# A longer pause of MLP work between a batch's first stage and its middle stage

## The chip, the cores and the metric

The kernel runs on one core of a Trainium2 chip. The metric is the device time of one execution in microseconds (us). A core has a matrix engine (TensorE, PE in the profile, its weight loads PEld), a vector engine (VectorE, DVE), a scalar engine (ScalarE, ACT), GpSimd (POOL) and SyncE (SP), which issues DMAs; ScalarE issues some as well.

## The reference

For each of 8 batches a sequence of 3008 tokens of 256 features goes through a Fourier transform, a complex projection with a soft threshold, and the inverse transform; all 24064 tokens then go through an MLP of width 2048 with a leaky ReLU.

```python
X = np.fft.rfft(x, axis=1)                 # x: 8 x 3008 x 256
Yr = Xr @ w_r - Xi @ w_i + b_r
Yi = Xr @ w_i + Xi @ w_r + b_i
Yr = np.sign(Yr) * np.maximum(np.abs(Yr) - lam, 0.0)   # and Yi
y = np.fft.irfft(Y, n=x.shape[1], axis=1)
h = y.reshape(24064, 256) @ w_in           # w_in: 256 x 2048
out = np.maximum(0.01 * h, h) @ w_out      # w_out: 2048 x 256
```

## The kernel before

The transform of 3008 = 47 x 64 points is split into stages. The first stage (`fwd(b)`) transforms along the 47: it loads x, folds it on GpSimd (sum and difference, lines 245 and 246), splits it into a high and a low part (lines 254 and 255), multiplies (line 78, tile psf from xz), copies the result out on ScalarE (line 264) and stores it to a DRAM tile u_dram from ScalarE's queue (line 267). The middle stage (`mid(b)`) loads u from u_dram on SyncE's queue (line 329), transforms along the 64 (line 343, bank psf from fb and u), projects and thresholds (line 78 with wr, wn, wd; VectorE lines 390 to 392), turns back (line 78 with gb) and stores to v_dram. A middle stage has 12 such rounds. The last stage (`inverse`, line 480) loads vin and gives the tokens y, which `forms` turns into seven combinations (yt, yc; lines 509 to 513) with high and low parts (line 505 on ScalarE, line 506 on VectorE).

The MLP takes the tokens in 47 chunks of 512, each in 8 steps, so 376 MLP steps. A step's first product is a seven-product scheme in two halves (`moe_a`, `moe_b`; line 92, banks psh, 21 matmuls of 256 columns) and its second product adds 12 matmuls of 512 columns two steps later (line 576, bank pso). Between the halves VectorE adds up what the first half left in the banks: line 543 (u2), line 545 and line 546 (gf). The third product of the second half writes into a bank that line 546 has read, so TensorE must wait for line 546 there. Line 557 ends the hidden tile gf and line 563 takes its low part gl.

Every matmul is done in three terms (high x high, high x low, low x high). While the MLP of one batch's tokens runs, the transform of a later batch is interleaved: a `Stream` wraps the generator of a stage, whose `yield` values say how many columns of work were just written, and after each half of an MLP step the main loop lets the current streams go on until their share of the whole is reached:

```python
work = frac / 0.95 * sum(s.total for s in streams)
for s in streams:
    s.to(work / s.total)
    work = max(0, work - s.total)
```

For a later batch the two streams are `fwd(b)` and then `mid(b)`. `mid(b)` writes the loads of its first two u tiles and then yields a number with no work behind it (line 424), so that MLP work is written until the stream's share has grown by that number. This is the pause.

All this sets the order in which the instructions are written. The order in which they stand on each engine is made from it by the library's scheduler, which works with a timed model of its own (`schedule_with_timeline_sim=True`); only the MLP's matmuls are tied to each other in their written order (`in_order`). The numbers in tile names count up in the written order.

Of the kernel before, what the change touches and what calls it, by code (L numbers as in the profile page):

```python
# [30 lines left out]
def spectral_mlp_kernel(  # L31
# [17 lines left out]
    NB = x.shape[0]  # L49
# [8 lines left out]
    CS = 512  # L58
# [253 lines left out]
    def mid(b):  # L312
# [13 lines left out]
        def load(j):  # L326
            u = sb.tile([P, 2, D], F32, name="u", tag="u", bufs=3)
            for c in range(2):
                ld = sync.dma_start(u[c * N2:(c + 1) * N2], ud[c, 2 * j:2 * j + 2, :N2, :].rearrange("k n d -> n k d"))
                if b == 0:  # L330
                    reads.append(ld)
            u_t[j] = u
# [88 lines left out]

        for j in range(2):
            load(j)
        yield 6 * CS if b else 0
        if b:
            for s in range(NPAIR):
                if s + 2 < NPAIR:
# [216 lines left out]
    MID = NPAIR * (16 * P + 18 * D + 3 * CS)  # L644
# [37 lines left out]
    with tc.issue_after(turned[0].ins):  # L682
        split_consts()
    m0 = Stream(mid(0), MID)
    m0.to(0.001)
    for c in range(2, 4):
# [28 lines left out]
    next(wout)  # L715


    mids = [Stream(mid(b), MID + 6 * CS) for b in range(1, NB)]
    cur, streams = -1, ()
    for i, pos in enumerate(moe()):  # L720
        if i % 2 == 0 and len(converted) < NQ:
# [121 lines left out]
```

## Time and profile before

| | |
|---|---|
| median of 3 timed runs (range) | 2605.85 us (2603.67 to 2608.62) |
| the profiled execution: time, span | 2600.34 us, 2598.6 us |
| TensorE matmul busy, share of the span | 2537.5 us, 98% |
| VectorE, ScalarE, GpSimd busy | 1897.1 us (73%), 1668.5 us (64%), 229.6 us (9%) |
| mean granted TensorE clock | 0.993 |
| chain that ended last: lines 576, 92, 78 | 38%, 34%, 11% |

The span reaches from the first to the last instruction. A share of busy time is an average over the whole; where a single wait stands, and who ended it, is read from the views of waits, of the chain that ended last, and of the timeline. The granted clock is the share of full speed that TensorE had.

### The profile page before, as it was taken

How to read it: one execution, taken by the hardware profiler on the slowest of the kernel's cores; microseconds unless marked ns; L12 is line 12 of the kernel's file. 1: busy time of each engine (PE TensorE's matmuls, PEld its weight loads, DVE VectorE, ACT ScalarE, POOL GpSimd, SP SyncE). 2: the span in 40 equal slices, each digit the busy share in tenths (PEclk: the TensorE clock that was granted, in tenths of full speed). 3: DMA queues.
4: the chain of work that ended last, by engine and by line, in shares of the span. 5: the costliest groups of instructions: out<-in, count | busy, mean ns of one | idle time of the engine just before them, and what ended most of it. 6: DMA issues, size and time to landing. Idle time of an engine off the chain costs nothing.

```text
span 2598.6 us, 42643 instructions
## 1 busy us (share of the span) xinstructions
PE 2537.5 (98%) x16300; PEld 2281.5 (88%) x16300; DVE 1897.1 (73%) x3403; ACT 1668.5 (64%) x3174; POOL 229.6 (9%) x180
## 2 busy tenths in 40 slices
PE   5999999999999999999999999999999999999999
PEld 4689888999889998899988999889998889999998
DVE  7687786776777778777786777877777777767675
ACT  5766665776556666567665666566666667655564
POOL 0001121100110001100021000210002000000000
PEclk8999999999999999999999999999999999999999
DMA  8621132111221113211132111321113221101000
GB/s 259 179 85 50 48 89 72 54 47 48 82 78 49 45 41 90 75 55 51 33 97 68 49 49 37 104 67 49 49 36 101 64 58 48 44 17 32 9 17 17
DMA packets 119912, 165.13 MB, mean 64 GB/s; under 512 B 13601, under 2 KB 69917, under 8 KB 119709
## 3 DMA queue, kind: packets, MB, share of 16 engines
q1 hardware_dynamic: 79120, 115.55, 14.6%
q10 hardware_dynamic: 40589, 46.87, 7.1%
q8 instruction: 128, 2.10, 0.4%
q14 instruction: 75, 0.61, 0.1%
HBM read 86.60 MB, written 75.76 MB: 62 GB/s over the span
## 4 chain that ended last, share of the span: by engine, by line
PE 89%; DVE 3%; DMA 2%; ACT 1%; issue 0%; ACTq 0%; SPq 0%; DVEq 0%
PE pso L576 38%; PE psh L92 34%; PE psf L78 11%; PE psf L480 3%; PE psf L343 3%; DMA u<-u_dram 1%; DMA u_dram<-xin 1%; DVE yl L506 0%; DVE gl L563 0%; DMA raw<-w_out_dram 0%; DVE gf L557 0%; ACT gh L561 0%; DVE yt L511 0%; ACT gf L559 0%; DVE yc L512 0%
## 5 line engine op out<-in xcount | busy, mean ns | idle before, releaser
L92 PE MATMUL psh<-yh,win_hi 128*128 128x256 f32 x2632 | 752.3, 286 | 13.8 <-DVE gf L546 10.6
L92 PE MATMUL psh<-yl,win_hi 128*128 128x256 f32 x2632 | 738.3, 280 | 0.6 <-DVE yl L506 0.5
L92 PE MATMUL psh<-yh,win_lo 128*128 128x256 f32 x2632 | 737.9, 280 | 0.0
L576 PE MATMUL pso<-gh,wout_hi 128*128 128x512 f32 x1504 | 593.9, 395 | 0.0
L576 PE MATMUL pso<-gl,wout_hi 128*128 128x512 f32 x1504 | 591.1, 393 | 0.5 <-DVE gl L563 0.5
L576 PE MATMUL pso<-gh,wout_lo 128*128 128x512 f32 x1504 | 590.4, 393 | 0.0
L563 DVE TENSOR_TENSOR gl<-gf,gh 128x1024 fp32r<-128x1024 f32 x376 | 471.8, 1255 | 92.7 <-ACT gh L561 90.6
L92 PEld LDWEIGHTS psh<-yh,win_hi 128*128 128x128 f32 x2632 | 497.0, 189 | 30.7 <-DVE gf L546 15.4
L92 PEld LDWEIGHTS psh<-yl,win_hi 128*128 128x128 f32 x2632 | 497.0, 189 | 12.5 <-DVE yl L506 1.0
L92 PEld LDWEIGHTS psh<-yh,win_lo 128*128 128x128 f32 x2632 | 496.6, 189 | 0.2
L557 DVE TENSOR_TENSOR gf<-psh,u 128x512 f32<-128x512 f32 x376 | 259.1, 689 | 256.3 <-PE psh L92 255.1
L561 ACT CAST gh<-gf 128x1024 fp32r<-128x1024 f32 x376 | 396.4, 1054 | 7.1
L559 ACT ACTIVATE gf<-gf 128x768 f32<-128x768 f32 x376 | 320.0, 851 | 49.5 <-DVE gf L557 47.7
L576 PEld LDWEIGHTS pso<-gl,wout_hi 128*128 128x128 f32 x1504 | 282.5, 188 | 62.9 <-DVE gl L563 1.0
L576 PEld LDWEIGHTS pso<-gh,wout_hi 128*128 128x128 f32 x1504 | 283.1, 188 | 46.9 <-ACT gh L561 0.4
L576 PEld LDWEIGHTS pso<-gh,wout_lo 128*128 128x128 f32 x1504 | 282.9, 188 | 44.9
L556 ACT ACTIVATE gf<-psh 128x256 f32<-128x256 f32 x376 | 145.5, 387 | 266.6 <-PE psh L92 246.9
L542 ACT COPY p<-psh 128x256 f32<-128x256 f32 x376 | 140.1, 373 | 220.2 <-PE psh L92 219.1
L379 POOL TENSOR_TENSOR kb<-bias,kc 128x512 f32<-128x512 f32 x84 | 119.0, 1417 | 1530.6 <-ACT kc L376 1409.6
L543 DVE TENSOR_TENSOR u<-psh,p 128x256 f32<-128x256 f32 x376 | 158.6, 422 | 105.8 <-ACT p L542 103.5
L545 DVE TENSOR_TENSOR gf<-psh,u 128x256 f32<-128x256 f32 x376 | 159.3, 424 | 29.7 <-PE psh L92 2.0
L546 DVE TENSOR_TENSOR gf<-psh,gf 128x256 f32<-128x256 f32 x376 | 159.1, 423 | 9.0
(134 smaller groups left out, 3253.2 us busy)
## 6 DMA issues: line engine op xcount, KB each, us to landing
u<-u_dram SPq DMA_DIRECT2D x192, 128.0 KB, 2.7
v_dram<-v ACTq DMA_DIRECT2D x192, 128.0 KB, 2.4
out_dram<-ob SPq DMA_DIRECT2D x94, 256.0 KB, 2.1
vin<-v_dram SPq DMA_DIRECT2D x96, 240.0 KB, 3.5
xin<-x_dram SPq DMA_DIRECT2D x90, 240.0 KB, 3.0
u_dram<-xin ACTq DMA_DIRECT2D x72, 240.0 KB, 2.4
u_dram<-xin SPq DMA_DIRECT2D x24, 240.0 KB, 3.9
raw<-w_out_dram SPq DMA_DIRECT2D x8, 512.0 KB, 5.0
```

The lines of the kernel that those rows point to most:

```text
L78: last = nc.tensor.matmul(dst, a, b, start=(i == 0), stop=(i == len(terms) - 1))
L92: mlp[:] = [nc.tensor.matmul(dst, a, b, start=start and i == 0, stop=i == 2, skip_group_check=True)]
L542: act.copy(p1, b1[:, lo])
L543: dve.tensor_add(u2, b1[:, hi], p1)
L545: dve.tensor_add(g[:, 3], b2[:, hi], u2)
L546: dve.tensor_add(g[:, 3], b2[:, lo], g[:, 3])
L556: act.activation(g[:, 0], b1[:, lo], AF.Prelu, alpha=SLOPE)
L557: dve.tensor_add(g[:, 1:3], b2.rearrange("p (k n) -> p k n", k=2), u2.unsqueeze(1).broadcast_to([P, 2, HT]))
L559: act.activation(g[:, 1:4], g[:, 1:4], AF.Prelu, alpha=SLOPE)
L561: cp = act.copy(gh, g)
L563: parted[:] = [cp, dve.tensor_sub(gl, g, gh.bitcast(F32))]
L576: mlp[:] = [nc.tensor.matmul(po, a[:, f, s], r[:, i], start=(f == 0 and j == 0), stop=(f == NF - 1 and j == 2),)]
```

## The change

The number that `mid(b)` yields between its first loads and its first work goes from 6 x 512 to 9 x 512 columns for every batch but the first, and the total of these streams goes up by as much. Nothing else is changed.

```diff
@@ -421,7 +421,7 @@
 
         for j in range(2):
             load(j)
-        yield 6 * CS if b else 0
+        yield 9 * CS if b else 0
         if b:
             for s in range(NPAIR):
                 if s + 2 < NPAIR:
@@ -715,7 +715,7 @@
     next(wout)
 
 
-    mids = [Stream(mid(b), MID + 6 * CS) for b in range(1, NB)]
+    mids = [Stream(mid(b), MID + 9 * CS) for b in range(1, NB)]
     cur, streams = -1, ()
     for i, pos in enumerate(moe()):
```

Since a scheduler makes the engines' order from the written one, three places of the built order are shown, before and after.

TensorE at the hand-over of the second later batch, from the last first-stage matmuls (fa1) to the first of the middle stage (fb). Before:

```order
L78 MATMUL psf_4147<-xz_4144,fa1_hi_233 120x256
L78 MATMUL psf_4147<-xz_4144,fa1_lo_234 120x256
L92 MATMUL psh_4510<-yh_3805,win_hi_186 128x256
L92 MATMUL psh_4510<-yl_3806,win_hi_186 128x256
...
L576 MATMUL pso_4280<-gh_4398,wout_hi_897 128x512
...
L576 MATMUL pso_4287<-gl_4400,wout_hi_897 128x512
L92 MATMUL psh_4510<-yh_3805,win_hi_186 128x256
L92 MATMUL psh_4510<-yl_3806,win_hi_186 128x256
L92 MATMUL psh_4510<-yh_3805,win_lo_187 128x256
L343 MATMUL psf_4246<-fb_103,u_4182 128x2x64 x4
```

The change:

```order
L78 MATMUL psf_4147<-xz_4117,fa1_hi_233 120x256
L78 MATMUL psf_4147<-xz_4117,fa1_lo_234 120x256
L92 MATMUL psh_4569<-yh_3821,win_hi_186 128x256
L92 MATMUL psh_4569<-yl_3822,win_hi_186 128x256
...
L576 MATMUL pso_4264<-gh_4475,wout_hi_897 128x512
...
L576 MATMUL pso_4287<-gl_4477,wout_hi_897 128x512
L92 MATMUL psh_4569<-yh_3821,win_hi_186 128x256
L92 MATMUL psh_4569<-yl_3822,win_hi_186 128x256
L92 MATMUL psh_4569<-yh_3821,win_lo_187 128x256
L343 MATMUL psf_4274<-fb_103,u_4182 128x2x64 x4
```

Between the pair of line 78 and line 343 stand 9 matmuls of line 92, 12 of line 576 and 3 of line 92 in both; the whole place has moved by one MLP step (psh_4510 is now psh_4569), and the bank of line 343 is written later (psf_4274 for psf_4246).

VectorE in MLP step 77 (near 670 us before), up to line 546. Lines 511, 512, 513 and 506 are the split of the next tokens, 390 to 392 the threshold of a middle stage. Before:

```order
L563 TENSOR_TENSOR gl_6911<-gf_6863,gh_6909 128x1024
L511 TENSOR_TENSOR yt_6913<-yc_6141,yt_6913 128x256
L512 TENSOR_TENSOR yc_6141<-yc_6141 128x256
L391 TENSOR_SCALAR c_6926<-t_6925 128x512
L543 TENSOR_TENSOR u2_6953<-psh_6938,p1_6952 128x256
L506 TENSOR_TENSOR yl_6915<-yc_6141,yh_6914 128x512
L513 TENSOR_TENSOR yc_6141<-yc_6141,yt_6913 128x256
L392 TENSOR_TENSOR t_6925<-t_6925,c_6926 128x512
L506 TENSOR_TENSOR yl_6915<-yt_6913,yh_6914 128x512
L545 TENSOR_TENSOR gf_6956<-psh_6939,u2_6953 128x256
L506 TENSOR_TENSOR yl_6915<-yc_6141,yh_6914 128x512
L546 TENSOR_TENSOR gf_6956<-psh_6939,gf_6956 128x256
```

The change:

```order
L513 TENSOR_TENSOR yc_6141<-yc_6141,yt_6913 128x256
L557 TENSOR_TENSOR gf_6863<-psh_6846,u2_6860 128x512
L506 TENSOR_TENSOR yl_6915<-yc_6141,yh_6914 128x512
L390 TENSOR_TENSOR t_6925<-psf_6884,kb_6802 128x512
L506 TENSOR_TENSOR yl_6915<-yt_6913,yh_6914 128x512
L506 TENSOR_TENSOR yl_6915<-yc_6141,yh_6914 128x512
L391 TENSOR_SCALAR c_6926<-t_6925 128x512
L543 TENSOR_TENSOR u2_6953<-psh_6938,p1_6952 128x256
L563 TENSOR_TENSOR gl_6911<-gf_6863,gh_6909 128x1024
L392 TENSOR_TENSOR t_6925<-t_6925,c_6926 128x512
L545 TENSOR_TENSOR gf_6956<-psh_6939,u2_6953 128x256
L546 TENSOR_TENSOR gf_6956<-psh_6939,gf_6956 128x256
```

The split (lines 513 and 506) has moved from behind line 543 to ahead of it; line 563 now stands behind line 543.

VectorE in MLP steps 123 and 124, at the split of another chunk. Before, in step 124:

```order
L557 TENSOR_TENSOR gf_10365<-psh_10348,u2_10362 128x512
L511 TENSOR_TENSOR yt_10419<-yc_9736,yt_10419 128x256
L512 TENSOR_TENSOR yc_9736<-yc_9736 128x256
L506 TENSOR_TENSOR yl_10421<-yc_9736,yh_10420 128x512
L513 TENSOR_TENSOR yc_9736<-yc_9736,yt_10419 128x256
L543 TENSOR_TENSOR u2_10448<-psh_10433,p1_10447 128x256
L506 TENSOR_TENSOR yl_10421<-yt_10419,yh_10420 128x512
L545 TENSOR_TENSOR gf_10451<-psh_10434,u2_10448 128x256
L563 TENSOR_TENSOR gl_10417<-gf_10365,gh_10415 128x1024
L546 TENSOR_TENSOR gf_10451<-psh_10434,gf_10451 128x256
```

The change, in step 123:

```order
L543 TENSOR_TENSOR u2_10362<-psh_10347,p1_10361 128x256
L511 TENSOR_TENSOR yt_10419<-yc_9736,yt_10419 128x256
L512 TENSOR_TENSOR yc_9736<-yc_9736 128x256
L506 TENSOR_TENSOR yl_10421<-yc_9736,yh_10420 128x512
L545 TENSOR_TENSOR gf_10365<-psh_10348,u2_10362 128x256
L513 TENSOR_TENSOR yc_9736<-yc_9736,yt_10419 128x256
L506 TENSOR_TENSOR yl_10421<-yt_10419,yh_10420 128x512
L546 TENSOR_TENSOR gf_10365<-psh_10348,gf_10365 128x256
```

The split of this chunk stands one step earlier and now lies between line 543 and line 546. The same five rows stand there in steps 29, 196 and 267 too, where before they did not.

## Rows read from the trace of the kernel before

**Rows 1.** Waits of TensorE from 140 us on: total us, times, longest.

```profile
PE psf L343 <- DMA u<-u_dram: 9.6, 6, 2.4
PE psh L92 <- DVE gf L546: 8.9, 8, 2.8
PE psh L92 <- DVE u L543: 2.2, 2, 1.9
```

**Rows 2.** Chain that ended last, 435 to 446 us: start, us, what.

```profile
436.06 1.05 PE psh L92 x9
437.11 0.25 PE psf L78 x2
...
437.39 0.38 ACT xin L264
...
437.80 3.10 DMA u_dram<-xin
...
440.91 2.75 DMA u<-u_dram
...
443.80 1.13 PE psf L343 x8
```

**Rows 3.** The same chain, 446 to 453 us.

```profile
446.24 3.25 PE psh L92 x18
449.49 2.74 PE pso L576 x12
```

**Rows 4.** TensorE in two stretches: us, busy (instructions), granted clock, DMA share, GB/s.

```profile
444.40:447.90 3.50, 3.50 (x22) 0.62 0.36 110
669.70:676.60 6.90, 4.22 (x19) 0.56 0.01 2
```

**Rows 5.** Timeline of TensorE near 670 us; in brackets the idle time before.

```profile
668.98 0.39 PE L92 MATMUL psh<-yh,win_hi 128*128 128x256 f32 x1 [1.91 <-DVE u L543]
...
672.38 0.58 PE L92 MATMUL psh<-yh,win_hi 128*128 128x256 f32 x1 [2.79 <-DVE gf L546]
```

**Rows 6.** Chain that ended last, 660 to 690 us.

```profile
665.41 1.44 DVE yt L511
666.85 1.41 DVE yc L512
...
668.59 0.33 DVE u L543
...
670.46 0.60 DVE yl L506
...
672.38 4.21 PE psh L92 x18
```

**Rows 7.** Timeline of GpSimd, 663 to 673 us.

```profile
664.57 2.00 POOL L245 TENSOR_TENSOR xs<-xin,xin 120x512 f32<-120x512 f32 x1 [9.65 <-DMA xin<-x_dram]
666.64 1.33 POOL L246 TENSOR_TENSOR xin<-xin,xin 120x512 f32<-120x512 f32 x1
```

**Rows 8.** All of line 511: ns least/median/most, first and last start, form.

```profile
L511 DVE TENSOR_TENSOR yt<-yc,yt x47: 412/420/1521, 127.1 to 2519.7; 128x256 f32<-128x256 f32 x47
```

**Rows 9.** Waits of TensorE, 200 to 430 us.

```profile
PE psf L78 <- ACT eh L358: 1.6, 2, 1.1
```

**Rows 10.** Waits of TensorE, 1150 to 1690 us.

```profile
PE psh L92 <- DVE gf L546: 2.0, 2, 1.2
```

**Rows 11.** Waits of TensorE, 2065 to 2120 us.

```profile
PE psh L92 <- DVE gf L546: 1.1, 1, 1.1
PE psh L92 <- DVE yl L506: 0.5, 1, 0.5
PE psf L78 <- ACT eh L358: 0.3, 1, 0.3
```

**Rows 12.** Timeline in an MLP step without a split: line 546, then the product behind it.

```profile
1594.94 0.43 DVE L546 TENSOR_TENSOR gf<-psh,gf 128x256 f32<-128x256 f32 x1
...
1597.70 0.28 PE L92 MATMUL psh<-yh,win_hi 128*128 128x256 f32 x1
```

## The prediction

> **What bounds the kernel now.** I read first who waits on TensorE once the opening 140 us are over. TensorE is the bound: it runs one long row of matmuls, and what can be won lies in the gaps of that row. The list of its waits [rows 1] is short: 9.6 us in six waits of line 343 for the tile u, and 8.9 and 2.2 us in ten waits of the MLP product (line 92) for VectorE's gf and u2 additions. So I look at two places: the hand-over from a batch's first stage to its middle stage, where the pause stands, and the worst VectorE wait.
>
> The hand-over of the second later batch is in the chain of waits [rows 2]: the last first-stage matmuls end at 437.36 (437.11 + 0.25), ScalarE copies them out from 437.39, its store to u_dram lands after 3.10 us, only then can SyncE issue the load of u, which takes 2.75 us, and the first middle-stage matmul starts at 443.80. From 437.36 to 443.80 that is 6.4 us of latency. In that time TensorE had 9 + 3 matmuls of line 92 (1.05 us for nine [rows 2]) and 12 of line 576 (2.74 us for twelve [rows 3]), so 1.05 + 0.35 + 2.74 = 4.1 us, and stood for the rest. The six waits of line 343 are this place in the six later batches. After it the granted clock was 0.62 on average over the next 3.5 us [rows 4], a mix of the 1.2 and 2.4 GHz levels, and 18 matmuls of line 92 took 3.25 us [rows 3] where 18 at 1.05 us for nine take 2.1: 1.1 us more.
>
> The second place is around 670 us. TensorE stood 1.91 and 2.79 us in one MLP step [rows 5], and the chain of waits there runs through VectorE [rows 6]: it did the additions of the inverse transform's split (yt, yc, yl) ahead of and between the additions that TensorE needed. After it the clock was granted at 0.56 over 6.9 us [rows 4], and 18 matmuls took 4.21 us [rows 6], 2.1 us more than 2.1.
>
> **The change, part by part.** It adds no instruction: both orders hold the same matmuls. It adds 3 x 512 = 1536 to the pause that a later batch's `mid` reports and the same to its total.
>
> *The pause itself.* By the code one would expect 3.7% of a stretch where 2.5% stood (4608 of 124928 units, 3072 of 123392), so more MLP between store and use, and the u waits gone. The built order says otherwise. Between the last first-stage matmul and the first of line 343 stand 9, 12 and 3 MLP matmuls before, and 9, 12 and 3 after (first pair of order rows, and the same in all six later batches). The numbers in the names, which count up as the code is written, tell why: in both versions the bank of line 343 (psf_4246, now psf_4274) was written ahead of the MLP bank that executes before it (psh_4510, now psh_4569). The scheduler already holds line 343 back until it believes that u has landed; a pause that ends earlier than that is not seen. So I cost this part at nothing: the six waits stay, 9.6 us, and the 1.1 us of slow clock with them. The bounds are 0 and 9.6 + 1.1 = 10.7 us gained.
>
> *The pacing.* The larger total lets every stretch spread its work a little differently. Counted in the order by MLP steps (376 in all), the attention's instructions move by mostly 0 and at most 2 steps, the last middle stage ends 0.3 step earlier, and the MLP's tail is unchanged. TensorE's work stays; only which VectorE and ScalarE rows meet which MLP step changes. What can change is therefore the waits of line 92 (and those of line 78 for ScalarE) at places whose neighbourhood is reordered.
>
> *What goes.* At these places the rows around the wait are no longer the same: 1.6 us near 312 and 343 us [rows 9], 1.91 + 2.79 us near 670 [rows 5], 2.0 us in two near 1152 and 1683 [rows 10], 1.1 + 0.5 + 0.3 us from 2070 to 2115 [rows 11]. Together 10.2 us, and 2.1 us of slow clock after the pair near 670: 12.3 us. At the largest the new order is plainly kinder (second pair of order rows): before, five attention operations stood between line 543 and line 546; now only lines 563 and 392 do, since the split is done earlier.
>
> *What comes.* TensorE waits when VectorE has much to do between line 543 and line 546 of one step. A step without such work has 2.3 us to spare: line 546 ended at 1594.94 + 0.43 and TensorE wanted it at 1597.70 [rows 12]. I counted in both orders the steps with at least 1.7 us of attention work there, by the durations of its rows. Before there are 12 that are now different, after there are 9 that are new. Of the 12, three waited: the pair near 670 (4.7 us), 1.2 near 1152 [rows 10], 1.1 near 2115 [rows 11], so 7.0 / 12 = 0.58 us a place; without the pair 2.3 / 11 = 0.21. Nine new places then cost 9 x 0.21 = 1.9 to 9 x 0.58 = 5.3 us. Four of the nine are one pattern (third pair of order rows): lines 511, 512, 506, 513 and 506 in that gap, three of 0.33 us (by line 543, which is as wide) and two of 0.60 [rows 6], 2.2 us, about the 2.3 to spare, so near nothing each. I still take 5.3, since what made the dear place dear, below, is not removed by the change. The other waits that go (10.2 - 7.0 = 3.2 us) I let come back in full at other places: they are many small chances that the change draws anew. New waits: 8.5 us. Bounds: 0, and 9 x (4.7 + 2.1) = 61 if each were as dear as the dearest, which the eleven others exclude; three such, 20.4 + 3.2 = 23.6, is as far as I go.
>
> *Why one place was so dear.* The two operations of lines 511 and 512 took 1.44 and 1.41 us on the chain [rows 6], against a median of 0.42 [rows 8]. In just that time GpSimd ran its two additions that fold the next batch's input, 664.57 to 666.57 and 666.64 to 667.97 [rows 7], and each VectorE operation ended 0.3 us behind one of them. That is 2 x 1.05 = 2.1 of the 4.7 us. The Trainium skill (page "SBUF — State Buffer", section "Who interferes with whom") says that a VectorE instruction with two SBUF inputs and a GpSimd one that reads SBUF exclude each other, and that the later one waits until the first has finished. The trace agrees here: the VectorE operations end with GpSimd's, rather than slow down by some share.
>
> The sum against the profiled execution's own time: 2600.34 - 12.3 + 8.5 = 2596.5 us. The three timed runs have a median of 2605.85, 5.5 above that execution, so on them 2605.85 - 3.8 = 2602.05 us.
>
> **The rivals.** (1) *The pause works on the chip as the code reads*: TensorE gets more to do before line 343 and the u waits end: 2605.85 - 10.7 = 2595.2. For it speaks only the code; the order, with the same 24 matmuls between, speaks against it.
> (2) *The dear place goes and nothing like it comes*: the new waits are 1.9 + 3.2 = 5.1, so 12.3 - 5.1 = 7.2 us gained, 2598.7; with no new waits at all 2593.6. For it speaks that the split near 670 is now ahead of line 543, and that four of nine new places fit into the spare time.
> (3) *Slower: the split meets GpSimd again.* Each meeting of a step's split with a fold costs up to 2.1 us on VectorE and, where the spare time is used up already, the whole 4.7 + 2.1 = 6.8 us. Three such places among the nine give 20.4 + 3.2 - 12.3 = 11.3 us, 2617; it is slower than no change by over 0.2% from 12.3 + 5.2 = 17.5 us of new waits. For it speaks that the pattern of line 511 behind line 543 stands in four steps where it stood in none, and uses up the spare 2.3 us; against it that two of the four lie in the midst of a middle stage, where no fold runs. By the rule cited above from the Trainium skill, such a meeting costs all that is left of GpSimd's instruction, so a place is either dear or free; this widens the case and does not move it.
>
> **How the numbers follow.** A timing of this kernel tells about 0.2%, 5.2 us, from no change. Forecast (reordered waits, a net of some -4 us, its own range 2600.6 to 2611): 0.50. Rival 1: 0.05. Rival 2: 0.32, nearly all of it over the 5.2 us. Rival 3: 0.13. So faster 0.37, same 0.50, slower 0.13. The forecast's time is 2602.05; the range leaves out a tenth on each side: from 2594, rival 2 with hardly a new wait, to 2611, where new waits are 17.5 us.
>
> **What would show it.** In the profile after, line 343 should again wait six times for u, about 9 to 11 us in all; if that is under 3 us, rival 1 holds. The pair of waits near 670 us should be gone or under 2 us. The waits of line 92 behind VectorE should sum to 6 to 12 us where 11.1 stood; under 5 is rival 2, over 20 rival 3, with VectorE's lines 509 to 513 at over 1 us beside GpSimd's additions. Wrong would be the whole reasoning if the time moved by over 0.3% with these sums unchanged, for instance by TensorE's clock alone.

## The result: no faster, slightly slower

| | before | change |
|---|---|---|
| median of 16 runs each (range) | 2602.13 us (2600.03 to 2608.62) | 2607.75 us (2604.26 to 2611.39) |
| the profiled execution: time, span | 2600.34, 2598.6 us | 2608.53, 2606.7 us |
| TensorE matmul busy, share of the span | 2537.5 us, 98% | 2541.6 us, 98% |
| mean granted TensorE clock | 0.993 | 0.992 |

The ratio of the two kernels is taken as 1.0018 with a 95% interval of 1.0011 to 1.0026: 4.7 us (0.0018 x 2602) slower, between 2.9 and 6.8; the two medians lie 5.6 us apart. That is under the 0.2% that the prediction took as what a timing can tell, but 16 runs of each tell it from no change. The forecast was 3.8 us faster.

The waits of TensorE in the changed kernel, from 140 us on (total us, times, longest), are to be held against [rows 1]:

```profile
PE psh L92 <- DVE gf L546: 8.2, 8, 2.5
PE psf L343 <- DMA u<-u_dram: 7.1, 6, 1.4
PE psf L78 <- ACT eh L358: 3.5, 4, 1.8
PE psh L92 <- DVE u L543: 2.7, 3, 1.3
PE psh L92 <- DVE yl L506: 2.3, 2, 1.4
PE psf L78 <- DVE eh L359: 0.9, 1, 0.9
PE pso L576 <- DVE gl L563: 0.8, 2, 0.5
PE psf L78 <- ACT v L418: 0.7, 1, 0.7
```

[rows 1] show only the three largest groups of before; the same list of before goes on with

```profile
PE psf L78 <- ACT eh L358: 1.8, 3, 1.1
...
PE psh L92 <- DVE yl L506: 0.5, 1, 0.5
```

and line 576 for gl with 0.5. Line 343 still waits six times for u, and its longest wait is 1.4 us where 2.4 stood. Small groups of before have grown: line 92 for yl, and line 78 for eh, which ScalarE writes (line 358) in the middle stage's own chain of copies. New are line 78 for eh from VectorE (line 359) and for v.

The hand-over of the second later batch, in the chain that ended last (start, us, what), answers to [rows 2]:

```profile
446.55 0.25 PE psf L78 x2
...
447.24 2.15 DMA u_dram<-xin
449.41 2.58 DMA u<-u_dram
452.12 1.13 PE psf L343 x8
```

The same steps take 5.3 us from the last matmul of line 78 (446.80) to the first of line 343, where 6.4 stood; the store landed after 2.15 us instead of 3.10. The work between is the same 24 matmuls in both built orders. Near 670 us, in the chain behind [rows 6], the split is shorter but still there:

```profile
670.10 2.84 DVE yl L506 x2
...
673.28 0.33 DVE u L543
...
675.72 0.44 DVE gf L546
676.20 4.21 PE psh L92 x18
```

Two operations of line 506 take 2.84 us together, where [rows 6] have 0.60 for one, and push line 543 and line 546 back; TensorE waits 0.92 us for the one and 1.91 for the other, 2.8 instead of 4.7 us, and the 18 matmuls behind them still run slowly, in 4.21 us as in [rows 6].

And this is new, at the start of a chunk of tokens; the timeline of TensorE from 460 to 475 us (in brackets the idle time and what ended it) has two waits:

```profile
465.31 0.39 PE L92 MATMUL psh<-yl,win_hi 128*128 128x256 f32 x1 [0.81 <-DVE yl L506]
467.38 0.58 PE L92 MATMUL psh<-yl,win_hi 128*128 128x256 f32 x1 [1.45 <-DVE yl L506]
```

So do the two largest of the late places, TensorE's timeline from 2110 to 2125 and from 2220 to 2234 us:

```profile
2119.45 0.39 PE L78 MATMUL psf<-wr_hi,eh 128*128 128x256 f32 x1 [1.83 <-ACT eh L358]
...
2227.34 0.39 PE L92 MATMUL psh<-yh,win_hi 128*128 128x256 f32 x1 [1.30 <-DVE u L543]
2228.43 0.39 PE L78 MATMUL psf<-wr_hi,eh 128*128 128x256 f32 x1 [0.47 <-ACT eh L358]
2230.32 0.38 PE L78 MATMUL psf<-wn_hi,eh 128*128 128x256 f32 x1 [0.68 <-ACT v L418]
```

**Where the time is.** Line 546 runs once in each of the 376 MLP steps, so its start is a common mark. It starts 3.9 us later in the first step of the changed kernel's profile and 4.6 us later in the eighth (184.14 against 179.55 us). Up to there the engines still run the same order, so that part is between two executions, not between two kernels. In the last step it is 8.2 us later (2593.30 against 2585.07). The change's own part of the profiled pair is so 8.2 - 4.6 = 3.6 us, in line with the timed 4.7. TensorE from the eighth mark to the last (us, busy (instructions), granted clock, DMA share, GB/s), before and with the change:

```profile
179.55:2585.07 2405.52, 2384.55 (x15595) 1.00 0.19 55
184.14:2593.30 2409.16, 2386.89 (x15593) 1.00 0.19 55
```

Its idle time grew by 1.3 us (22.27 for 20.97), as do its waits from 170 us on (22.5 us after, 21.2 before). The other 2.3 us (2386.89 - 2384.55) are busy time: the same matmuls held TensorE longer. The slow clock doesn't explain it, since it costs 5.1 us in both (one minus the granted clock, summed over stretches of 10 us from 170 us on). In the profile a single matmul of line 92 lasts 0.28 us [rows 12], while nine in a row take 1.05 us [rows 2], so short stalls can lie inside busy time; which matmuls took longer, and why, no row shows.

### The profile page after: what moved, and what is told of

Its sections match the earlier page's. It is cut to its first block, busy times and chain, and to the rows that moved or that the text cites. A ratio compares the mean times of both kernels' runs of the same rounds, so it can differ in the third digit from the quotient of the medians.

```text
span 2606.7 us, 42619 instructions
## 1 busy us (share of the span) xinstructions
PE 2541.6 (98%) x16300; PEld 2282.6 (88%) x16300; DVE 1888.5 (72%) x3403; ACT 1662.2 (64%) x3174; POOL 234.6 (9%) x180
## 4 chain that ended last, share of the span: by engine, by line
PE 87%; DVE 3%; ACT 2%; DMA 2%; issue 1%; POOL 0%; ACTq 0%; SPq 0%; DVEq 0%; POOLq 0%
PE pso L576 37%; PE psh L92 33%; PE psf L78 11%; PE psf L480 3%; PE psf L343 3%; DVE yl L506 1%; DMA u<-u_dram 1%; DMA u_dram<-xin 1%; DVE gl L563 0%; ACT gf L559 0%; DVE gf L557 0%; DVE t L390 0%; ACT yh L505 0%; ACT zf L400 0%; ACT yc L493 0%
## 5 line engine op out<-in xcount | busy, mean ns | idle before, releaser
L563 DVE TENSOR_TENSOR gl<-gf,gh 128x1024 fp32r<-128x1024 f32 x376 | 465.2, 1237 | 95.0 <-ACT gh L561 93.5
```

Of the source, the lines that this page charges most:

```text
L563: parted[:] = [cp, dve.tensor_sub(gl, g, gh.bitcast(F32))]
```

## The experiments

Theory A: the pause is a number that changes the written order; the scheduler makes another order from it, and waits go and come at places that have nothing to do with the pause. Then the time follows the list of waits, and other small changes of the numbers move it either way. Theory B: a longer pause costs by itself (MLP work that stands before the middle stage is missing later), so more pause is slower, and its two edits add up. All kernels compute the whole result. Diffs are against the kernel before unless said. The kernels were timed in three groups, each with its own runs of the kernel before, whose medians are 2604.75 us for e1 to e4, 2603.61 for p3 to p24 and 2603.01 for f1 to f4; the ratios are within a group. The waits are those of one profiled execution of each kernel.

| kernel | ratio to before (95%) | waits of TensorE from 170 us on | of these, line 343 |
|---|---|---|---|
| before | 1 | 21.2 us | 9.6 |
| change | 1.0018 (1.0011 to 1.0026) | 22.5 | 7.1 |
| e1: pause alone | 0.9986 (0.9978 to 0.9994) | 18.6 | 7.9 |
| e2: total alone | 0.9977 (0.9969 to 0.9986) | 16.8 | 7.2 |
| e3: first later batch only | 1.0011 (1.0002 to 1.0019) | 24.7 | 8.3 |
| e4: all later batches but the first | 1.0027 (1.0016 to 1.0038) | 24.6 | 9.9 |
| p3: 3 x 512 | 1.0005 (0.9996 to 1.0014) | 21.6 | 9.2 |
| p8: 8 x 512 | 1.0000 (0.9991 to 1.0009) | 21.4 | 9.1 |
| p12: 12 x 512 | 1.0015 (1.0006 to 1.0024) | 22.6 | 6.2 |
| p24: 24 x 512 | 0.9981 (0.9972 to 0.9989) | 16.7 | 2.6 |
| f1: change, other pace | 1.0015 (1.0006 to 1.0024) | 23.4 | 8.0 |
| f3: before, other pace | 0.9996 (0.9987 to 1.0005) | 20.6 | 9.8 |
| f2: change, no additions on GpSimd | 1.0094 (1.0080 to 1.0108) | 32.8 | 8.9 |
| f4: middle stage held back | 1.0009 (1.0000 to 1.0018) | 17.7 | 0.5 |

Over the 14 kernels the ratio and the sum of waits go together with a correlation of 0.93 (0.83 without f2, the farthest of them).

**e1, the pause alone; e2, the total alone.**

```diff
 e1
-        yield 6 * CS if b else 0
+        yield 9 * CS if b else 0
 e2
-    mids = [Stream(mid(b), MID + 6 * CS) for b in range(1, NB)]
+    mids = [Stream(mid(b), MID + 9 * CS) for b in range(1, NB)]
```

> Pause 9 x 512, total left at 6 x 512. Theory A (the order is drawn anew): within 0.25% of before, either sign, with waits of TensorE at places of its own. Theory B (the longer pause costs by itself): 4 to 5 us slower than before.

> Pause left at 6 x 512, total 9 x 512: only the pacing. Theory A: within 0.25% of before, either sign. Theory B: no change to before, within 0.1%.

Measured: 2601.62 us and 2598.81 us. Each half of the change is faster than before, by 0.14% and 0.23%, and both together are slower by 0.18%. Costs that add up can't do that. In e1 the waits of line 343 are 7.9 us, as with the change, so it is not there that the two part. In e2 the place near 670 us is nearly free; the waits of TensorE from 430 to 700 us in e2:

```profile
PE psf L343 <- DMA u<-u_dram: 2.3, 1, 2.3
PE psh L92 <- DVE yl L506: 0.9, 1, 0.9
PE psh L92 <- DVE gf L546: 0.8, 1, 0.8
```

That is 4.0 us, where the same stretch of the changed kernel has 6.3 (2.3 + 1.9 + 1.2 + 0.9) and that of before 7.0 (2.8 + 2.3 + 1.9). In the profiled executions of e1 and e2 the clock costs nothing from 170 us on, by the same sum that gave 5.1 us; the last section says how much of their gain this may be.

**e3 and e4, the change for one group of batches only.**

```diff
 e3
-        yield 6 * CS if b else 0
+        yield (9 if b == 1 else 6) * CS if b else 0
-    mids = [Stream(mid(b), MID + 6 * CS) for b in range(1, NB)]
+    mids = [Stream(mid(b), MID + (9 if b == 1 else 6) * CS) for b in range(1, NB)]
 e4: the same with (6 if b == 1 else 9) in both lines
```

> Pause and total 9 x 512 in the first later middle stage alone, 6 x 512 in the six others. Theory A: what the change loses up to about 500 us (the waits for yl at the start of the seventh chunk, 2.3 us and 1.7 us of slow clock) can come here too, if the order there is the same as in the change: 2 to 5 us slower. Theory B: a seventh of the loss, 0.7 us.

> Pause and total 9 x 512 in the six later stretches, 6 x 512 in the first. Theory A: no waits for yl near 465 us, since that part stands as before; the rest drawn anew, within 0.25% of before. Theory B: six sevenths of the loss, 4 us slower.

Measured: 2607.51 and 2611.36 us, 0.11% and 0.27% slower; their sum of 0.38% is not the change's 0.18%. But place by place they are its two halves. e3 has the change's early waits; its waits of TensorE from 460 to 475 us:

```profile
PE psh L92 <- DVE yl L506: 2.3, 2, 1.5
```

and before's late ones, its waits from 2070 to 2140 us, row for row [rows 11]:

```profile
PE psh L92 <- DVE gf L546: 1.1, 1, 1.1
PE psh L92 <- DVE yl L506: 0.5, 1, 0.5
PE psf L78 <- ACT eh L358: 0.3, 1, 0.3
```

e4 has no wait from 460 to 475 us and the change's late ones; its waits from 2070 to 2140 and from 2220 to 2240 us:

```profile
PE psf L78 <- ACT eh L358: 1.8, 1, 1.8
...
PE psh L92 <- DVE u L543: 1.3, 1, 1.3
PE psf L78 <- ACT v L418: 0.7, 1, 0.7
PE psf L78 <- ACT eh L358: 0.5, 1, 0.5
```

So a wait for VectorE or ScalarE belongs to its piece of the order and comes back to a tenth of a microsecond in another kernel with the same piece. What the place at 460 to 475 us costs can't be read this way: line 546 starts 7.1 us later than before in e3's 49th MLP step and 11.2 us in its 61st, but only 4.8 and 5.7 us in the changed kernel, which has the same two waits and a fall of the clock behind them; e3 has a third wait in between, 1.4 us for eh.

e3 holds a test that is worth more. From the 101st step on its instructions on TensorE, VectorE and ScalarE stand in the same order as those of before, one by one (by line and tile), so that this is one order in two executions. TensorE from the 101st start of line 546 to the last, before and in e3:

```profile
825.07:2585.07 1760.00, 1749.72 (x11448) 1.00 0.18 52
835.96:2595.63 1759.67, 1749.74 (x11448) 1.00 0.18 52
```

The busy time is the same to 0.02 us, so the 2.3 us more of it in the changed kernel is far more than two executions of one order differ by here: it goes with the order, as the waits for VectorE and ScalarE do. The waits for u do not: before has 2.4 us near 1405 us, where its store landed after 3.52 us, and e3 has 1.4 us at the same place of the order (1415 us), with 2.27 us for the store.

**p3, p8, p12 and p24, other lengths.**

```diff
-        yield 6 * CS if b else 0
+        yield 3 * CS if b else 0
-    mids = [Stream(mid(b), MID + 6 * CS) for b in range(1, NB)]
+    mids = [Stream(mid(b), MID + 3 * CS) for b in range(1, NB)]
 p8, p12 and p24: 8, 12 and 24 in both lines
```

> Pause and total of 3 x 512 instead of 6 x 512. Theory A (the time differs only because the order around the MLP steps is drawn anew): within 0.25% of before, either sign; the six waits for u stay at 7 to 10 us in all, since 4.18 us of MLP matmuls stand in the hand-over as before. Theory B (a longer pause squeezes the middle stage, about 1.6 us for each 512 by the change of 4.7 us for three): 4.7 us faster than before, ratio 0.998.

> Pause and total of 8 x 512. Theory A: within 0.25% of before, either sign, and not tied to the change's 0.18%; waits for u at 7 to 10 us. Theory B: 3.1 us slower than before, ratio 1.0012, between before and the change.

> Pause and total of 12 x 512. The built order has 4.72 us of matmuls in the hand-over in five of six later batches where 4.18 stood, so theory A expects the waits for u to fall by about 5 x 0.54 = 2.7 us, to 5 to 7 us, and the time to be within 0.3% of before. Theory B: 9.4 us slower, ratio 1.0036.

> Pause and total of 24 x 512. The built order has 5.61 us of matmuls in five hand-overs where 4.18 stood, so theory A expects the waits for u to fall by 5 x 1.43 = 7 us, to 1 to 3 us, and the time to be 0 to 8 us below before apart from the order drawn anew (ratio 0.995 to 1.001). Theory B: 28 us slower, ratio 1.011.

Measured for 3, 6, 8, 9, 12 and 24 x 512: +0.05, 0, 0.00, +0.18, +0.15 and -0.19%. No trend of B's kind goes through these. What does follow the length is the hand-over, and only from 12 on. In the built order the matmuls between the last of line 78 and the first of line 343 come to 4.18 us in all six later batches at 3, 6, 8 and 9 x 512; to 4.72 us in five of them at 12, and to 5.61 in five at 24. With that the waits of line 343 fall from some 9 us over 6.2 to 2.6. The chain that ended last in p24, 445 to 456 us:

```profile
448.27 0.24 PE psf L78 x2
448.51 0.89 PE psf L480 x8
449.40 1.07 PE psh L92 x9
450.47 1.62 PE pso L576 x7
452.09 0.89 PE psf L480 x8
452.98 1.16 PE pso L576 x5
454.14 1.00 PE psf L343 x8
```

Here the chain stays on TensorE from line 78 to line 343, with 16 matmuls of line 480 in place of three of line 92; where the changed kernel waited, nothing waits. The other waits of p24 went up from 11.6 (21.2 - 9.6) to 14.1 us, so it wins 4.5 of the 7.0 us in waits, and 4.9 us in the timed runs (0.0019 x 2603.6).

**f1 and f3, another pace.** The divisor that sets the share of all stretches moves by a thousandth, in the change (f1) and in the kernel before (f3).

```diff
-        work = frac / 0.95 * sum(s.total for s in streams)
+        work = frac / 0.951 * sum(s.total for s in streams)
```

> The change as it is (pause and total 9 x 512), and the divisor of the pacing 0.951 instead of 0.95, which has nothing to do with the pause. Its order is the change's up to MLP step 12 and differs after it. Theory A (the time comes from the waits that the order draws): ratio anywhere in 0.997 to 1.003, with the waits at 2119 and 2227 us or 465 us there or not there by the order, so probably closer to before than the change is, 1.000 with a spread of 0.002. Theory B (the longer pause costs): 1.0018, as the change.

> Before (pause and total 6 x 512) with the divisor of the pacing 0.951 instead of 0.95. Same order as before up to MLP step 23. Theory A: ratio to before in 0.997 to 1.003, a spread like that of the kernels with another pause. Theory B: 1.000 within 0.0007.

Measured: 1.0015 and 0.9996, as far apart as the change and before. That is what B expects and not what I had hoped for from A: the two loose ends of this redraw did not bring the pair together. It is no proof of B: 1.0015 lies in A's range too, and f1's sum of waits came out near the change's (23.4 and 22.5 us) by other waits. f1 keeps the change's early places, among them the pair of 0.81 and 1.45 us for yl at 466 and 468 us; but near 670 us it has 1.1 us instead of 2.8, none of the waits at 2119 us and of line 92 at 2227, and 1.2 us near 720 and 1.4 near 1520 that the change has not. So f1 doesn't decide. B falls by e1, e2, p8 and p24.

**f2, no additions on GpSimd.** Against the changed kernel, to test the reason that the prediction gave for the dear place:

```diff
-            eng = pool if b else dve
+            eng = dve
-                    pool.tensor_add(kb, bias, kc.unsqueeze(1).broadcast_to([P, 2, D]))
+                    dve.tensor_add(kb, bias, kc.unsqueeze(1).broadcast_to([P, 2, D]))
```

> The change with the folds and the kb additions on VectorE instead of GpSimd: nothing left that VectorE can meet, for about 168 additions more on VectorE. If the meetings make the waits (about half of the 14.6 us behind the opening lie within 8 us behind a slowed VectorE operation), the pair near 675 us falls from 2.8 to under 1 us and the waits apart from u to 6 to 10 us; the time 0 to 8 us below the change, ratio to before 0.999 to 1.002. If the meetings don't matter and the VectorE load does, waits rise over 15 us and the ratio over 1.003.

Measured: 2627.42 us, 0.94% slower. VectorE's busy time grew from 1888.5 to 1953.9 us and the waits to 32.8. The slowed operations are gone: of line 511 none takes over 427 ns, where the changed kernel has one of 1078 and before one of 1521 [rows 8], and of line 563 none over 1227, where the changed kernel has one of 2321. All of line 511 in f2 (ns least/median/most):

```profile
L511 DVE TENSOR_TENSOR yt<-yc,yt x47: 414/418/427, 130.1 to 2546.9; 128x256 f32<-128x256 f32 x47
```

But a wait of 2.7 us for line 546 stays near the place (686.6 us), where under 1 us was expected if the meetings make the waits. The chain that ended last there, from line 543 to line 546:

```profile
683.66 0.42 DVE yc L513
684.08 0.60 DVE t L392
684.68 0.60 DVE yl L506
685.29 0.33 DVE gf L545
685.62 0.60 DVE yl L506
686.22 0.34 DVE gf L546
```

Four operations of the attention at their usual length, 2.22 us (0.42 + 3 x 0.60), stand between line 543 and line 546 and make up most of the 2.7 us. The meeting with GpSimd makes operations longer; that it makes the wait is not shown. Nor is f2 a clean test, since its order is another one and VectorE has more to do: waits over 15 us and a ratio over 1.003 were expected for that case, and both came.

**f4, the first round of a middle stage tied into the MLP's order.** For the later batches from the second on, the written order of line 343's first round is made binding, with a pause of 30 x 512 ahead of it, so that MLP work does stand before it.

```diff
-        yield 6 * CS if b else 0
+        yield 30 * CS if b else 0
-                stage_b(s)
+                in_order(stage_b, s) if b > 1 and s == 0 else stage_b(s)
-    mids = [Stream(mid(b), MID + 6 * CS) for b in range(1, NB)]
+    mids = [Stream(mid(b), MID + 30 * CS) for b in range(1, NB)]
```

> Pause and total 30 x 512, and the first round of line 343 in each of the six later batches tied behind the MLP matmul written just before it, so that the scheduler can't draw it forward. The built order has 5.61, three times 9.47, 14.71 and 4.72 us of matmuls in the six hand-overs where 4.18 stood before. The chain from the last first-stage matmul to the landing of u was 5.2 to 6.4 us long, so the waits for u fall from 9.6 to under 2.5 us. Theory A: 5 to 8 us faster from that, give or take 5 us of waits drawn anew: ratio 0.995 to 1.000. Theory B: 38 us slower, ratio 1.014.

Measured: 2605.23 us, 0.09% slower with an interval that reaches to no change, where 5 to 8 us less was expected. No wait for u is left, and over half of that gain is given back: the other waits went from 11.6 to 17.2 us, 6.6 of them line 78 for eh (two between 2160 and 2230 us are 4.4 us long together). Its sum of waits is still 3.5 us below before's while its time is not: it is the kernel that the sum misplaces most. Between the eighth and the last start of line 546 (183.38 to 2589.41 us) its TensorE is idle 3.3 us less than before's and busy 3.8 us longer (2388.36 against 2384.55), with the same 5.1 us for the clock: the rest of the gain goes there.

## Why the prediction was wrong, step by step

*The pause itself* was right: costed at nothing because the scheduler holds line 343 back by its own model. Six waits stay, and p12 and p24 show where a pause begins to be seen: with 9 x 512 and less the hand-over's 24 matmuls don't change. Rival 1, for which under 3 us was the sign, did not come. The six waits sum to 7.1 us where 9 to 11 was forecast, because the two long ones of before were short (1.2 and 1.4 us for 2.3 and 2.4): their stores landed after 2.15 and 2.25 us instead of 3.10 and 3.52. By the pair of before and e3 above, the second of these is a difference between executions, not one that the pause makes. These 2.5 us of luck made the miss smaller.

*The pacing* was right in that the order is redrawn in small and waits move. That TensorE's work stays was taken to mean that its time stays; the matmuls are the same, but they took 2.3 us longer. The sum had no term for it.

***What goes* is the step that failed most.** It counted 12.3 us, 6.8 of them (4.7 + 2.1) at the place near 670 us, since only lines 563 and 392 now stand between line 543 and line 546. The split was done earlier, but there it met GpSimd's additions, and line 543 and line 546 came late all the same: the pair shrank only to 2.8 us, and the slow clock behind it stayed (4.21 us for 18 matmuls again). The wait near 1683 us (0.84) stands at 1687 with 0.97. The waits near 312 and 343, near 1152 and from 2070 to 2115 us are gone. So of the 12.3 us only 6.4 went (10.2 - 2.8 - 0.97, and nothing of the slow clock): 5.9 us of the miss.

***What comes* failed too, in its rule more than in its size.** It allowed 8.5 us, 5.3 of them for nine new steps with 1.7 us or more of attention work between line 543 and line 546. The waits at places without one before sum to 10.3 us, but of the nine only one had a wait of line 92, 0.35 us near 783 us, where before had 0.36; that the size was near is luck. (The prediction says that three of the twelve such steps of before waited; by its rule the step near 783 us is a fourth.) What came was of kinds that the rule doesn't see: 2.3 us for yl at the start of a chunk; line 78 for eh and v, 5.1 us (3.5 + 0.9 + 0.7) where 1.8 stood; and line 92 at other steps (1.30 us at 2227, 1.07 at 378). The waits of line 92 for gf and u2 sum to 10.9 us (8.2 + 2.7), inside the 6 to 12 that were forecast where 11.1 stood, so that this sign did not tell the forecast from the result. The spare time of [rows 12] was right for the pattern of line 511, which was free as argued. But a rule that was made from the waits of before looks only where before had waited.

Put together, -6.4 + 10.3 - 2.5 = 1.4 us of waits (1.3 by the lists, as a wait of 0.3 us near 272 us went too) and 2.3 us of busy time give the 3.6 us of the profiled pair, where -12.3 + 8.5 = -3.8 was forecast. One fall of the clock went with the hand-over near 444 us and one came behind the waits for yl, so the clock's cost did not change.

*Why one place was so dear*: the meeting with GpSimd is real as a slowing. Line 511's longest goes from 1.08 us in the changed kernel to 0.43 in f2, where GpSimd does no additions. Near 670 us in the changed kernel it is line 506 that meets the fold:

```profile
669.41 1.29 POOL L245 TENSOR_TENSOR xs<-xin,xin 120x512 f32<-120x512 f32 x1 [9.18 <-PE psh L92]
670.78 1.62 POOL L246 TENSOR_TENSOR xin<-xin,xin 120x512 f32<-120x512 f32 x1
```

against VectorE's timeline in the same stretch:

```profile
670.02 1.23 DVE L506 TENSOR_TENSOR yl<-yt,yh 128x512 fp32r<-128x512 f32 x1
671.17 1.77 DVE L506 TENSOR_TENSOR yl<-yc,yh 128x512 fp32r<-128x512 f32 x1
```

The first ends at 671.25, 0.55 us behind line 245, the second at 672.94, 0.54 behind line 246. By the rule of the Trainium skill that the prediction cited (page "SBUF — State Buffer", section "Who interferes with whom") the later of two such instructions waits for the first to finish; the trace agrees again: what lies behind GpSimd's end, 0.55 and 0.54 us, is about the 0.60 us that such an operation takes by itself [rows 6]. As the cause of the wait it was not shown: f2 has a wait of 2.7 us without it.

*Rival 3* named the right sign by the wrong mechanism: none of the nine places among which it put its three dear ones had a wait of line 92 over 0.4 us; the meeting that was there stayed, at 2.8 us. And the sum was made with a certainty that it didn't have: the edits tried here, f2 apart, moved the time between -0.23 and +0.27%, and the forecast of -3.8 us lay well inside that. That 2607.75 us still lies in the range of 2594 to 2611 owes more to its width, and to a base of three runs whose median was 3.7 us above that of sixteen (2605.85, 2602.13), than to the reasoning.

What stays open: why the same matmuls keep TensorE busy 2.3 us longer with the change, and 3.8 us longer in f4. Why the two halves of the change make kind orders and the whole an unkind one has no reason beyond the order itself: no single wait was put back or taken out by hand.

## What to carry to other kernels

Where a scheduler with a model of its own makes the order, read in the built order whether a written pause changes the place that it is meant for; below what the model already holds back, it does nothing there and redraws the rest. Such a redraw moved this kernel by a quarter of a per cent either way, so forecast it near zero with that width, and if the time matters try several neighbours: e2, the total alone, is the fastest found (0.9977, with p24 at 0.9981 inside its interval), by its order and not by its idea. Waits are not the whole of it: hold TensorE's busy time and idle time between the same two marks side by side. When counting new waits, count at every place where the bound engine takes something from another one (the start of a chunk, the attention's own chain), not at the kind of place that waited before.

## What the runs showed that I had not expected

The granted clock does not follow from the waits alone. In the changed kernel the pair of waits for yl (0.81 and 1.45 us) was followed by a fall; in the execution of e1 that was profiled the same pair, 0.81 and 1.46 us before 462.62 and 464.69 us, was not. TensorE in a stretch of 7 us around the pair (us, busy (instructions), granted clock, DMA share, GB/s), in the changed kernel:

```profile
464.00:471.00 7.00, 4.74 (x20) 0.76 0.13 37
```

and in e1:

```profile
461.00:468.00 7.00, 4.73 (x28) 1.00 0.13 37
```

The busy time is the same, 4.74 and 4.73 us, but at full speed 28 matmuls fit into it and with a clock of 0.76, a mix of the 1.2 and 2.4 GHz levels, only 20. The kernel before shows it too: 2.3 us of waiting brought 0.62 in [rows 4], and a wait of 2.4 us near 1405 us nothing:

```profile
1402.00:1409.00 7.00, 4.56 (x38) 1.00 0.38 108
```

So a gap of this size may or may not cost 1.7 us more ((1 - 0.76) x 7.00), and part of a kernel's difference of a few microseconds hangs on it: from 170 us on the clock cost 5.1 us in the profiled executions of before, the change and e3, and nothing in those of e1 and e2.

The timed runs bear this out. The mean clock of a run goes from 0.991 to 0.995 over the 31 runs of before in the first group, so it differs from execution to execution of one kernel. It averages 0.9934 in the runs of e1 and 0.9933 in those of e2, against 0.9919 in before's. Over 2600 us such a difference of 0.0015 is an estimated 3.9 us: it can be all of e1's gain (0.0014 x 2604.75 = 3.6 us) over half of e2's (6.0 us), and, with 0.9932 against 0.9922, half of p24's (4.9 us). It doesn't save theory B, which wants e1 4 to 5 us slower. Nor is the clock alone the time: f1 and p12 ran at 0.9935 and 0.9931, against 0.9925 and 0.9922 for before, and were slower, and the change ran at 0.9924.
